# A dense layer whose first three token tiles share one pass over the weights, with float64 weights decoded in that pass

## The chip, the core and the metric

The kernel runs on one core of one Trainium2 chip. A core has five engines that each work through their own queue in order: TensorE (PE, whose weight loads are shown apart as PEld), VectorE (DVE), ScalarE (ACT), GpSimd (POOL) and SyncE (SP), which here only issues DMAs. They wait for each other by semaphores. The metric is the device time of one execution in microseconds (us).

## The reference, cut to what matters

```python
attn_out = _attn_ref(q, k, v)                    # 4 x 8 heads x 576 x 64, two sparse masks
x = attn_out.transpose(0, 2, 1, 3).reshape(2304, 512)
# experts: each token with x @ w_skip > 0 goes to the one expert with the largest logit
for e in range(8):                               # w1: 8 x 512 x 1024, w2: 8 x 1024 x 512, float32
    h = np.maximum(xc[mask] @ w1[e], 0.0)
    y[mask] = gate_w[mask, None] * (h @ w2[e])
out[do_compute] = xc + y
# dense layer, all 2304 tokens; w_in 512 x 2048 and w_out 2048 x 512 are float64
h = x @ w_in
g = np.maximum(0.01 * h, h)
return (g @ w_out).astype(np.float32)
```

## The kernel before, in words

The program has three stages: attention with the router, the experts, and the dense layer.

**Products.** Every float32 operand of a product is split into a high part (type fp32r) and a low part (the rest), and three products are added: high by high, high by low, low by high. One step of an expert or of the dense layer takes 128 hidden columns (a chunk f) and 256 tokens. `mm1` makes the hidden values `ph` in PSUM from 12 products of 256 columns, and `mm2` adds 6 products of 512 columns into the outputs `po` (experts) or `pf` (dense layer). PE's order is written by hand: `mm1` of step j, then `mm2` of step j - 2 (LAG = 2). `ph` has two buffers, so `mm1` of step j + 2 can't begin before the readers of `ph` of step j are done.

**Experts.** An expert has 8 chunks, so there are 64 steps. For each step SP loads a piece of w1 and of w2 (256 KB each). ACT makes the high parts (L495, L504), DVE the low part of w1 (`l1`, L498) and POOL the low part of w2 (`l2`, L507). Of `ph`, ACT makes `gh` (L596) and DVE makes `gl` (L597, which reads `ph` in PSUM and `gh` in SBUF). `split_rows` turns the 256 token rows of the next expert once per expert. `expert_out` adds the result to the rows (L602) and POOL scatters them to memory (L604); POOL also gathers the rows (L541). `last_out` passes the last expert's part straight into the dense layer's first rows.

**Decoding.** The dense weights are float64 and are turned into float32 parts on the chip. There are 64 jobs, four for each of the 16 chunks of the dense layer (two of w_in, two of w_out), in the chunks' order. A job has four steps: SP loads 256 KB (`raw`, three buffers); ACT takes the absolute of the high words into `w` (L128, two buffers); DVE does four operations on `w` (L133 to L136); ACT copies the high part (L141) and POOL subtracts it for the low part (`lo`, L142). Each call of `decode_tick` moves every job under way by one step and lets a new one enter. Six jobs enter during attention. The other 58 enter beside the experts, one in each step from the third on (`DEC_MOE`), and `decode_ready(15)` finishes them all ahead of the dense layer.

**Dense layer.** Nine tiles of 256 tokens are done one after the other, 16 steps each, so the weights are gone through nine times. In a step, ACT makes `t = 0.01 ph` (L737), DVE `g = max(t, ph)` (L739), ACT `gh` (L742) and DVE `gl = g - gh` (L743, where `g` and `gh` both lie in SBUF). The rows of the next tile are loaded in its fifth step and split in its tenth.

The order on the engines other than PE is set by the scheduler of the language, with the first operation of each decode step put behind the PE instruction that stands there in the program.

## Time and profile before

| what | us |
|---|---|
| median of 3 runs (lowest to highest) | 868.01 (867.65 to 873.32) |
| span of the profiled execution, first to last instruction | 859.5 |
| median of the runs less that span | 8.5 |
| attention and router | 192.3 |
| experts, to the dense layer's first product | 253.1 |
| dense layer and last outputs | 414.1 |

The profile is of one execution. Its page gives busy time by engine over the whole span, and the views named below give it by stage, by line and in order of time. Busy time alone doesn't say what a stage waits for: an engine that is busy can be held by another in the middle of an instruction, and then the duration of that instruction is long. So the durations of one kind of instruction are given both as a mean and as lowest, median and highest.

### The profile page before, as it was taken

The numbers are of one execution on the slowest core, as the hardware profiler recorded it, in microseconds if no ns is written. First come the engines' busy times: TensorE is split into PE (matmuls) and PEld (weight loads), VectorE is DVE, ScalarE is ACT, GpSimd is POOL, SyncE is SP. The second block draws the span as 40 slices with busy tenths as digits, with TensorE's granted clock in tenths as the row PEclk, the third lists the DMA queues.
The fourth block names the chain that finished last, engine by engine and source line by source line (L and its number), as shares of the span: only waits on it lengthen the run. The fifth ranks groups of instructions, "written<-read, shape, count | busy, mean of one in ns | idle before, by whom it ended". The sixth has DMA issues, their size and how long they took to land.

```text
span 859.5 us, 14337 instructions
## 1 busy us (share of the span) xinstructions
PE 768.2 (89%) x5090; PEld 681.4 (79%) x5090; DVE 473.3 (55%) x1247; ACT 359.3 (42%) x940; POOL 184.8 (21%) x203
## 2 busy tenths in 40 slices
PE   7885699859888788788889999999999999999998
PEld 6874599838766666676669899999999999999897
DVE  3552187758999999999973323232323232323222
ACT  5453165636465465565543333333333333333322
POOL 0010001125676676676640000000000000000000
PEclk9897688979999999999999999999999999999999
DMA  8994389768766676676521000000000000000000
GB/s 203 229 224 131 117 213 236 205 171 262 219 215 206 208 225 209 201 226 209 179 78 49 24 25 26 26 25 26 25 26 25 25 1 25 1 25 2 24 2 25
DMA packets 83108, 98.28 MB, mean 114 GB/s; under 512 B 8124, under 2 KB 55790, under 8 KB 83029
## 3 DMA queue, kind: packets, MB, share of 16 engines
q1 hardware_dynamic: 80468, 93.12, 37.4%
q0 software_dynamic: 2560, 4.18, 1.6%
q8 instruction: 41, 0.67, 0.3%
q14 instruction: 39, 0.31, 0.1%
HBM read 85.41 MB, written 16.09 MB: 118 GB/s over the span
## 4 chain that ended last, share of the span: by engine, by line
PE 58%; DVE 19%; DMA 14%; issue 5%; ACT 2%; POOL 1%; SPq 1%; DVEq 0%; ACTq 0%; POOLq 0%
PE ph L583 25%; PE pf L591 23%; DVE l L498 4%; DMA tt<-in_tl 4%; DMA xs_d<-xo 4%; DVE w L135 3%; PE sc L284 3%; DVE w L133 3%; DVE w L134 2%; DVE w L136 2%; DVE gl L597 2%; PE o L318 2%; DMA kb<-x_d,idx 2%; PE po L591 1%; DMA qb<-in_qs 1%
## 5 line engine op out<-in xcount | busy, mean ns | idle before, releaser
L739 DVE TENSOR_TENSOR g<-t,ph 128x256 f32<-128x256 f32 x144 | 60.6, 421 | 200.1 <-ACT t L737 200.0
L583 PE MATMUL ph<-th,winh 128*128 128x256 f32 x576 | 161.8, 281 | 0.2 <-ACT th L574 0.2
L583 PE MATMUL ph<-tl,winh 128*128 128x256 f32 x576 | 161.0, 280 | 0.3 <-DVE tl L575 0.3
L583 PE MATMUL ph<-th,winl 128*128 128x256 f32 x576 | 160.4, 278 | 0.0
L737 ACT ACTIVATE t<-ph 128x256 f32<-128x256 f32 x144 | 55.3, 384 | 205.4 <-PE ph L583 205.3
L591 PE MATMUL pf<-woutl,gh 128*128 128x512 f32 x288 | 114.1, 396 | 0.0
L591 PE MATMUL pf<-wouth,gl 128*128 128x512 f32 x288 | 114.1, 396 | 0.0
L591 PE MATMUL pf<-wouth,gh 128*128 128x512 f32 x288 | 113.7, 395 | 0.0
L583 PEld LDWEIGHTS ph<-tl,winh 128*128 128x128 f32 x576 | 108.1, 188 | 6.7 <-DVE tl L575 0.5
L583 PEld LDWEIGHTS ph<-th,winh 128*128 128x128 f32 x576 | 108.4, 188 | 6.3 <-ACT th L574 0.4
L583 PE MATMUL ph<-th,h 128*128 128x256 f32 x256 | 77.5, 303 | 37.9 <-DVE gl L597 37.3
L583 PEld LDWEIGHTS ph<-th,winl 128*128 128x128 f32 x576 | 108.3, 188 | 0.0
L743 DVE TENSOR_TENSOR gl<-g,gh 128x256 fp32r<-128x256 f32 x144 | 61.2, 425 | 70.0 <-PE pf L591 54.3
L583 PEld LDWEIGHTS ph<-th,h 128*128 128x128 f32 x256 | 49.3, 193 | 55.4 <-DVE gl L597 54.0
L507 POOL TENSOR_TENSOR l<-r,h 128x512 fp32r<-128x512 f32 x64 | 88.3, 1380 | 18.2 <-ACT h L504 5.0
L742 ACT CAST gh<-g 128x256 fp32r<-128x256 f32 x144 | 58.5, 407 | 66.2 <-DVE g L739 66.2
L583 PE MATMUL ph<-tl,h 128*128 128x256 f32 x256 | 73.2, 286 | 0.3 <-DVE tl L521 0.3
L583 PE MATMUL ph<-th,l 128*128 128x256 f32 x256 | 73.0, 285 | 0.0
L498 DVE TENSOR_TENSOR l<-r,h 128x512 fp32r<-128x512 f32 x64 | 60.6, 947 | 10.9 <-ACT h L495 6.1
L284 PE MATMUL sc<-kb,qb 128*96 128x128 f32 (+2 forms) x344 | 56.4, 316 | 9.4 <-DMA qb<-in_ql 3.5
L591 PEld LDWEIGHTS pf<-wouth,gl 128*128 128x128 f32 x288 | 54.1, 188 | 13.0
L290 ACT ACTIVATE p_t<-sc,mx 96x128 f32<-96x128 f32 (+2 forms) x172 | 48.6, 365 | 25.7 <-DVE mx L287 25.2
(116 smaller groups left out, 1422.8 us busy)
## 6 DMA issues: line engine op xcount, KB each, us to landing
r<-in_w SPq DMA_DIRECT2D x128, 256.0 KB
raw<-in_win SPq DMA_DIRECT2D x32, 256.0 KB
raw<-in_wout SPq DMA_DIRECT2D x32, 256.0 KB
kb<-x_d SPq DMA_DIRECT2D x18, 256.0 KB
out<-y SPq DMA_DIRECT2D x18, 256.0 KB
x_d<-xt SPq DMA_DIRECT2D x11, 384.8 KB
vt<-in_vl SPq DMA_DIRECT2D x12, 296.0 KB
kb<-in_kl SPq DMA_DIRECT2D x12, 256.0 KB
```

Of the source, the lines that this page charges most:

```text
L133: behind_pe(nc.vector.tensor_scalar(wf, wf, F32_MAX_HI, F32_MIN_HI, ALU.min, ALU.max))
L135: nc.vector.scalar_tensor_tensor(w, raw[:, :, 1], 0xC0000000, w, ALU.bitwise_and, ALU.bitwise_or)
L284: nc.tensor.matmul(sc[:, h, :], z["q"][:, h, :nq], z["k"][:, h, :], start=True, stop=True)
L290: nc.scalar.activation(p_t[:nq, h, :nk], sc[:, h, :], AF.Exp, bias=mx[:, h:h + 1], scale=scale)
L498: nc.vector.tensor_tensor(l1, r1, h1.bitcast(F32), ALU.subtract)
L507: nc.gpsimd.tensor_tensor(l2, r2, h2.bitcast(F32), ALU.subtract)
L583: nc.tensor.matmul(ph, a[:, c, :], x[:, c, :], start=(i == 0), stop=(i == n - 1))
L591: nc.tensor.matmul(po[t], a[:, s], x, start=(first and i == 0), stop=(last and i == 2))
L737: nc.scalar.mul(t1, ph, 0.01)
L739: nc.vector.tensor_tensor(g, t1, ph, ALU.max)
L742: nc.scalar.copy(gh, g)
L743: nc.vector.tensor_tensor(gl, g, gh.bitcast(F32), ALU.subtract)
```

## The change

The dense weights are held in one tile per chunk instead of one tile for all. The tiles of the first 8 chunks stand from the beginning; those of the last 8 are laid into the memory that the experts' tiles leave free. Only 16 of the 58 jobs enter beside the experts, one in every fourth step; the other 42 enter in the dense layer. There the first three token tiles go together: four steps of tile 0 come first (LEAD), and then each round has one step of tile 0, one of tile 1 and one of tile 2, the latter two four chunks behind. In the 48 steps of these tiles `decode_tick` is called once, once and twice in turn, so four jobs enter in a round of three steps, as many as one chunk needs. Tile 2 adds its outputs in the PSUM buffers that otherwise serve the row splits; the rows of tiles 1 and 2 are loaded at the beginning of the dense layer and split after its fourth step, one behind the other, and those of tile 3 are split in the buffers of `ph`. Tiles 3 to 8 run one after the other as before.

```diff
-DEC_MOE = set(range(2, 64))
-DEC_F = 15
+DEC_MOE = set(range(2, 64, 4))
+DEC_DENSE = (1, 1, 2)
+TRIO = 3
+EC = 8
+LEAD = 4
...
+    def weight_tiles(pool, lo, hi):
+        for n, nm in enumerate(("winh", "winl", "wouth", "woutl")):
+            for f in range(lo, hi):
+                dense_w[n, f] = pool.tile([P, KC, P] if n < 2 else [P, DM], F32R, tag=f"{nm}{f}", name=nm)
+
+    weight_tiles(big, 0, EC)
...
-    def split_rows(rows):
-        th = mp.tile([P, KC, NTT], F32R, tag="th", name="th")
-        tl = mp.tile([P, KC, NTT], F32R, tag="tl", name="tl")
+    def split_rows(rows, pool=ps_c, tag="c"):
+        th = tp.tile([P, KC, NTT], F32R, tag="th", name="th")
+        tl = tp.tile([P, KC, NTT], F32R, tag="tl", name="tl")
...
-    decode_ready(DEC_F)
...
+    ectx.close()
+    late = ctx.enter_context(tc.tile_pool(name="late", bufs=1, reuse_waits=RW))
+    weight_tiles(late, EC, FC2)
...
-    fseq = [(i, f) for i in range(NI) for f in range(FC2)]
+    fseq = [(0, f) for f in range(LEAD)]
+    for r in range(LEAD, FC2 + LEAD):
+        fseq += [(i, r if i == 0 else r - LEAD) for i in range(TRIO) if i or r < FC2]
+    n_trio = len(fseq)
+    fseq += [(i, f) for i in range(TRIO, NI) for f in range(FC2)]
+    rows = {i: load_rows(i) for i in range(1, TRIO)}
...
-                pos[i] = [ps_a.tile([P, DM], F32, tag="a", name=f"pf{t}") for t in range(2)]
-            if i == 0:
-                decode_ready(min(f + DEC_F, FC2 - 1))
+                pool, tag = (ps_c, "c") if i == TRIO - 1 else (ps_a, "a")
+                pos[i] = [pool.tile([P, DM], F32, tag=tag, name=f"pf{t}") for t in range(2)]
+            decode_ready(f)
...
+            if j == LEAD - 1:
+                for n in range(1, TRIO):
+                    xt_of[n] = split_rows(rows.pop(n))
...
+            if j < n_trio:
+                for _ in range(DEC_DENSE[j % len(DEC_DENSE)]):
+                    decode_tick()
```

On DVE, in the middle of the experts before (`l` the low part of w1, `gl` that of the hidden values, `w` the four operations of a decode job), two steps read:

```order
L498 TENSOR_TENSOR l_3708<-r_3613,h_3707 128x512
L597 SCALAR_TENSOR_TENSOR gl<-ph,gh 128x256
L133 TENSOR_SCALAR w<-w 128x256
L134 TENSOR_SCALAR w<-w 128x256
L135 SCALAR_TENSOR_TENSOR w<-raw,w 128x256
L136 SCALAR_TENSOR_TENSOR w<-raw,w 128x256
L498 TENSOR_TENSOR l_3753<-r_3658,h_3752 128x512
L597 SCALAR_TENSOR_TENSOR gl<-ph,gh 128x256
```

The same engine and stage of the change, over three steps:

```order
L141 TENSOR_SCALAR w<-w 128x256
L509 TENSOR_TENSOR l_4001<-r_3916,h_4000 128x512
L142 TENSOR_SCALAR w<-w 128x256
L608 SCALAR_TENSOR_TENSOR gl<-ph,gh 128x256
L143 SCALAR_TENSOR_TENSOR w<-raw,w 128x256
L144 SCALAR_TENSOR_TENSOR w<-raw,w 128x256
L509 TENSOR_TENSOR l_4036<-r_3961,h_4035 128x512
L608 SCALAR_TENSOR_TENSOR gl<-ph,gh 128x256
L509 TENSOR_TENSOR l_4087<-r_3996,h_4086 128x512
L608 SCALAR_TENSOR_TENSOR gl<-ph,gh 128x256
```

A job stood in nearly every step; now one stands in every fourth.

On DVE in the dense layer before, two steps (`g` the hidden values, `gl` their low part) read:

```order
L739 TENSOR_TENSOR g<-t_6277,ph 128x256
L743 TENSOR_TENSOR gl_6282<-g,gh_6281 128x256
L739 TENSOR_TENSOR g<-t_6298,ph 128x256
L743 TENSOR_TENSOR gl_6303<-g,gh_6302 128x256
```

The same engine in the shared pass of the change, about two steps:

```order
L758 TENSOR_TENSOR g<-t_6462,ph 128x256
L142 TENSOR_SCALAR w<-w 128x256
L143 SCALAR_TENSOR_TENSOR w<-raw,w 128x256
L762 TENSOR_TENSOR gl_6467<-g,gh_6466 128x256
L144 SCALAR_TENSOR_TENSOR w<-raw,w 128x256
L141 TENSOR_SCALAR w<-w 128x256
L142 TENSOR_SCALAR w<-w 128x256
L143 SCALAR_TENSOR_TENSOR w<-raw,w 128x256
L758 TENSOR_TENSOR g<-t_6499,ph 128x256
L144 SCALAR_TENSOR_TENSOR w<-raw,w 128x256
L141 TENSOR_SCALAR w<-w 128x256
L762 TENSOR_TENSOR gl_6504<-g,gh_6503 128x256
```

Decode operations now stand between `g` and `gl` of one step and between the steps.

On SP, at the beginning of the dense layer of the change (`kb` rows of tokens out of `x_d`, `raw` float64 weights to decode):

```order
L130 DMA raw<-in_win 128x2x256
L130 DMA raw<-in_wout 128x512
L545 DMA kb_125<-x_d 128x512 x2
L545 DMA kb_126<-x_d 128x512 x2
L130 DMA raw<-in_wout 128x512
L545 DMA kb_127<-x_d 128x512
L130 DMA raw<-in_win 128x2x256
```

The four loads of the rows of tiles 1 and 2, which read what the last expert scatters, stand ahead of the next loads for decoding.

## Rows read from the trace of the kernel before

**Rows 1.** Busy time by stretch, whole stages: us, busy by engine, PEclk, DMA share, GB/s.

```profile
0.00:192.30 192.30, 147.67 (x1192) 136.17 (x1192) 101.12 (x548) 87.84 (x295) 18.11 (x52) 0.83 0.75 192
192.30:445.40 253.10, 210.14 (x1243) 174.81 (x1243) 239.48 (x396) 140.08 (x324) 165.68 (x151) 0.97 0.66 206
445.40:859.50 414.10, 410.42 (x2655) 370.39 (x2655) 132.69 (x305) 131.38 (x322) 0.97 (x1) 1.00 0.07 22
```

**Rows 2.** Waits of the experts' stage: us in total, times, longest us.

```profile
PEld ph L583 <- DVE gl L597: 54.0, 41, 3.2
```

**Rows 3.** Chain of work that ended last, dense layer: start us, us, what.

```profile
451.22 1.40 PE ph L583 x12
452.62 1.40 PE pf L591 x6
...
851.65 4.21 PE pf L591 x18
```

**Rows 4.** Groups by line, experts: busy us, mean ns, idle before with releasers.

```profile
L135 DVE SCALAR_TENSOR_TENSOR w<-raw,w 128x256 uint32<-128x256 uint32 x58 | 46.7, 805 | 1.1
...
L134 DVE TENSOR_SCALAR w<-w 128x256 uint32<-128x256 uint32 x58 | 37.6, 648 | 1.3
...
L136 DVE SCALAR_TENSOR_TENSOR w<-raw,w 128x256 uint32<-128x256 uint32 x58 | 36.2, 623 | 0.5
L133 DVE TENSOR_SCALAR w<-w 128x256 f32<-128x256 f32 x58 | 30.2, 521 | 3.8 <-ACT w L128 3.8
...
L128 ACT ACTIVATE w<-raw 128x256 f32<-128x256 f32 x58 | 25.3, 436 | 10.1 <-POOL winl L142 4.7 <-POOL woutl L142 4.2 <-DMA raw<-in_wout 0.5
...
L141 ACT CAST wouth<-w 128x256 fp32r<-128x256 f32 x30 | 12.2, 406 | 45.9 <-DVE w L136 45.9
```

**Rows 5.** Single lines, experts: ns lowest/median/highest of one, first and last start.

```profile
L133 DVE TENSOR_SCALAR w<-w x58: 275/286/2472, 202.3 to 439.1; 128x256 f32<-128x256 f32 x58
L134 DVE TENSOR_SCALAR w<-w x58: 275/296/2132, 202.6 to 439.4; 128x256 uint32<-128x256 uint32 x58
L135 DVE SCALAR_TENSOR_TENSOR w<-raw,w x58: 406/426/2467, 202.9 to 439.7; 128x256 uint32<-128x256 uint32 x58
L136 DVE SCALAR_TENSOR_TENSOR w<-raw,w x58: 407/424/2092, 203.4 to 440.7; 128x256 uint32<-128x256 uint32 x58
L498 DVE TENSOR_TENSOR l<-r,h x61: 671/684/2899, 195.2 to 426.1; 128x512 fp32r<-128x512 f32 x61
L597 DVE SCALAR_TENSOR_TENSOR gl<-ph,gh x64: 406/411/425, 195.8 to 437.7; 128x256 fp32r<-128x256 f32 x64
L507 POOL TENSOR_TENSOR l<-r,h x63: 1262/1313/1808, 198.0 to 437.6; 128x512 fp32r<-128x512 f32 x63
L142 POOL TENSOR_TENSOR woutl<-w,wouth x30: 732/748/1200, 207.0 to 441.7; 128x256 fp32r<-128x256 f32 x30
```

**Rows 6.** Timeline of DVE and POOL, in an expert: start us, us, what.

```profile
329.99 2.46 DVE L135 SCALAR_TENSOR_TENSOR w<-raw,w 128x256 uint32<-128x256 uint32 x1
...
330.19 0.75 POOL L142 TENSOR_TENSOR woutl<-w,wouth 128x256 fp32r<-128x256 f32 x1
330.88 1.27 POOL L507 TENSOR_TENSOR l<-r,h 128x512 fp32r<-128x512 f32 x1
332.37 0.41 DVE L597 SCALAR_TENSOR_TENSOR gl<-ph,gh 128x256 fp32r<-128x256 f32 x1
```

**Rows 7.** The page's costliest groups, dense layer: busy us, mean ns, idle before.

```profile
L739 DVE TENSOR_TENSOR g<-t,ph 128x256 f32<-128x256 f32 x144 | 60.6, 421 | 200.1 <-ACT t L737 200.0
...
L743 DVE TENSOR_TENSOR gl<-g,gh 128x256 fp32r<-128x256 f32 x144 | 61.2, 425 | 70.0 <-PE pf L591 54.3
```

**Rows 8.** Timeline around the dense layer's beginning, engines PE, POOL and SP.

```profile
440.21 0.61 PE L552 MATMUL pts<-zero 128*128 128x512 bf16 x2
...
446.20 0.97 POOL L604 DMA_INDIRECT x_d<-kb,idx  x1 [2.45 <-DVE tl L575]
...
448.36 2.73 SPq L534 DMA_DIRECT2D kb<-x_d  x6
```

More of the change, by code (lines that the diff above doesn't have):

```diff
@@ L98, in tile_sparse_attention_moe_ffn @@
     x2_d = dp.tile([NT, XW], F32, name="x2_d")
-    winh = big.tile([P, KC, DFF], F32R, name="winh")
-    winl = big.tile([P, KC, DFF], F32R, name="winl")
-    wouth = big.tile([P, FC2, DM], F32R, name="wouth")
-    woutl = big.tile([P, FC2, DM], F32R, name="woutl")
+    dense_w = {}
+    def weight_tiles(pool, lo, hi):
[3 more added lines that the diff above has]
+    weight_tiles(big, 0, EC)
     DN = 256
@@ L140, in decode_step @@
             wf = sh(w.bitcast(F32))
+            hi, lo = dense_w[k, f][:, cols], dense_w[k + 1, f][:, cols]
             behind_pe(nc.scalar.copy(hi, wf))
@@ L508, in split_w2 @@
         return h2, l2
-    def split_rows(rows):
-        th = mp.tile([P, KC, NTT], F32R, tag="th", name="th")
-        tl = mp.tile([P, KC, NTT], F32R, tag="tl", name="tl")
+    def split_rows(rows, pool=ps_c, tag="c"):
+        th = tp.tile([P, KC, NTT], F32R, tag="th", name="th")
+        tl = tp.tile([P, KC, NTT], F32R, tag="tl", name="tl")
         for c2 in range(KC // 2):
-            pt = ps_c.tile([P, 2, NTT], F32, tag="c", name="ptx")
+            pt = pool.tile([P, 2, NTT], F32, tag=tag, name="ptx")
             for c in range(2):
@@ L565, in last_out @@
             gys.append((yh, yl))
-        th, tl = (mp.tile([P, KC, NTT], F32R, tag=n, name=n) for n in ("th", "tl"))
+        th, tl = (tp.tile([P, KC, NTT], F32R, tag=n, name=n) for n in ("th", "tl"))
         for t in range(2):
@@ L729, in tile_sparse_attention_moe_ffn @@
             if f == 0:
-                th, tl = xt_of.pop(i)
-                pos[i] = [ps_a.tile([P, DM], F32, tag="a", name=f"pf{t}") for t in range(2)]
-            if i == 0:
-                decode_ready(min(f + DEC_F, FC2 - 1))
-            fs = slice(f * P, (f + 1) * P)
-            ph = mm1(winh[:, :, fs], winl[:, :, fs], th, tl)
-            t1 = wp.tile([P, NTT], F32, tag="h2", bufs=HB2, name="t1")
+                pool, tag = (ps_c, "c") if i == TRIO - 1 else (ps_a, "a")
+                pos[i] = [pool.tile([P, DM], F32, tag=tag, name=f"pf{t}") for t in range(2)]
+            decode_ready(f)
+            ph = mm1(dense_w[0, f], dense_w[1, f], *xt_of[i])
+            if f == FC2 - 1:
+                xt_of.pop(i)
+            t1 = wp.tile([P, NTT], F32, tag="t1", bufs=HB2, name="t1")
             nc.scalar.mul(t1, ph, 0.01)
-            g = wp.tile([P, NTT], F32, tag="l2", bufs=HB2, name="g")
+            g = wp.tile([P, NTT], F32, tag="g", bufs=HB2, name="g")
             nc.vector.tensor_tensor(g, t1, ph, ALU.max)
-            gh = mp.tile([P, NTT], F32R, tag="gh", bufs=3, name="gh2")
-            gl = mp.tile([P, NTT], F32R, tag="gl", bufs=3, name="gl2")
+            gh = wp.tile([P, NTT], F32R, tag="gh", bufs=3, name="gh2")
+            gl = wp.tile([P, NTT], F32R, tag="gl", bufs=3, name="gl2")
             nc.scalar.copy(gh, g)
@@ L744, in tile_sparse_attention_moe_ffn @@
             gs[j] = gh, gl
-            if i + 1 < NI and f == 4:
-                rows[i + 1] = load_rows(i + 1)
         if j >= LAG:
@@ L757, in tile_sparse_attention_moe_ffn @@
                         for b in (1, 0):
-                            mm2(po, *gs[j - LAG - b], wouth[:, f - b, :], woutl[:, f - b, :], False, b == 0, (t,))
-                    y = wp.tile([P, DM], F32, tag=("h1", "l1")[t], bufs=HB, name="y")
+                            mm2(po, *gs[j - LAG - b], dense_w[2, f - b], dense_w[3, f - b], False, b == 0, (t,))
+                    y = wp.tile([P, DM], F32, tag=f"y{t}", bufs=2, name="y")
                     nc.scalar.copy(y, po[t])
@@ L763, in tile_sparse_attention_moe_ffn @@
             i, f = fseq[j]
-            if i + 1 < NI and f == 9:
-                xt_of[i + 1] = split_rows(rows.pop(i + 1))
+            if j == LEAD - 1:
+                for n in range(1, TRIO):
+                    xt_of[n] = split_rows(rows.pop(n))
+            if i >= TRIO - 1 and i + 1 < NI and f == 4:
+                rows[i + 1] = load_rows(i + 1)
+            if i >= TRIO - 1 and i + 1 < NI and f == 9:
+                xt_of[i + 1] = split_rows(rows.pop(i + 1), *((ps_b, "b") if i < TRIO else (ps_c, "c")))
+            if j < n_trio:
+                for _ in range(DEC_DENSE[j % len(DEC_DENSE)]):
+                    decode_tick()
 def _layout(inputs):
```

18 lines of the change are left out of this document (10 added, 8 removed).

## Prediction

> **What bounds the kernel now.** I read the busy time by stretch first, cut at the experts' first product and at the dense layer's [rows 1]. The dense layer is PE's: 410.4 of 414.1 us busy at the full clock. The experts are not: PE is busy for 210 of 253 us, and DVE for 239.5. The list of waits says the same: the weight load of `mm1` waits 54.0 us for `gl` [rows 2], an operation of DVE that frees the buffer of `ph`.
>
> Next, what PE needs where nothing holds it. In the dense layer a step takes 1.40 + 1.40 = 2.80 us [rows 3]. From the first product at 445.4 to 855.9 are 410.5 us, which is 144 steps (403.2 us) and 8 row splits, so a split costs 0.9 us. A step in an expert has the same 12 and 6 products, yet it takes 253.1/64 = 3.95 us.
>
> Then, why DVE is so busy. The groups by line give the four operations of a decode job as 521 + 648 + 805 + 623 ns = 2.60 us [rows 4], the single lines as 286 + 296 + 426 + 424 = 1.43 us by the median, with single ones up to 2.47 us [rows 5]. The timeline shows what happens in the long ones: L135 begins at 329.99 and ends at 332.45, and while it runs POOL does a `lo` and an `l2`, to 332.15; it ends 0.30 us after them [rows 6]. So DVE is held while POOL works, not slow. This befalls operations that take all operands from SBUF (L133 to L136, and `l1`, 0.68 us, up to 2.90) and not `gl`, which reads PSUM: 64 of them lie between 406 and 425 ns [rows 5].
>
> If those operations of DVE and POOL's subtractions can never run together, the experts need 64 x (0.684 + 1.313) + 58 x (1.432 + 0.748) = 127.8 + 126.4 = 254 us. The stage takes 253. I read this as its bound: not DVE alone, but DVE and POOL taking turns.
>
> **The change part by part.**
>
> *Experts.* Of 58 jobs about 15 stay. The turns come to 127.8 + 15 x 2.18 = 160.5 us, and PE's own work is longer: 64 x 2.80 = 179.2, 7 splits 6.3, and `last_out` from 440.2 to 445.4 [rows 8], 5.2: together 190.7 us. What remains of the wait for `gl` isn't shown anywhere: nothing at best; if it goes by the number of jobs, 54.0 x 15/58 = 14 us. DVE's order has three steps without a job behind one with a job, in which it can catch up, so I take the middle, 7. The stage is then 197.7 us, or **-55.4** (bounds -62.4 and -48.4).
>
> The loads don't take over: the stage moves 206 GB/s x 253.1 us = 52.1 MB now [rows 1], 43 jobs of 0.262 MB go away, and 40.8 MB in 197.7 us are 206 GB/s again, at which the DMA engines are busy for 0.66.
>
> *The shared pass.* A round of three steps needs 8.40 us of PE. DVE has three `g` and `gl` (421 and 425 ns, [rows 7]) and four jobs. Its price has two ends. Were DVE never held, it would be 3 x 0.846 + 4 x 1.43 = 8.26 us, hidden below PE's 8.40. Held as often as in the experts, it would be 2.54 + 4 x 2.60 = 12.9 us. Between them lies the turn-taking: four jobs with their `lo`, 4 x 2.18 = 8.72, and three `gl`. In the dense layer `gl` has both operands in SBUF, as `l1` has, so I count it as held too: + 1.28 = 10.0 us. `g` reads PSUM and goes beside POOL. I take 10.0, since this count gave the experts' 253 us. In the experts POOL's subtractions come to 2.06 us a step, the most of it in pieces of 1.31; here they are one of 0.75 us per job, so the price is nearer to the taking of turns than to 12.9.
>
> The Trainium skill ("SBUF — State Buffer", section "Who interferes with whom") says that a DVE instruction with two SBUF inputs waits for the whole of a GpSimd instruction that reads SBUF, and one with a single SBUF input doesn't. The rows of `l1` and of the experts' `gl` agree (2899 against 425 ns at most, [rows 5]); no run here shows the dense `gl` beside POOL. With the rule a round is 10.0 us, without it for `gl` 8.72, which over the pass would be 12 us less.
>
> 39 of the 44 jobs that DVE still has at the beginning fall into such rounds, 9.75 rounds. PE can't run ahead of DVE, because `mm1` waits for `g` two steps back. So the cost is 9.75 x (10.0 - 8.4) = **+15.6** (bounds 0 and 9.75 x 4.5 = +43.9). Behind the last job the steps go at 2.80 again.
>
> ACT is no bound: three `t` and `gh` and four times 0.436 + 0.406 [rows 4] are under 6 us a round. The weights are in time by the order of jobs: at the step that first needs chunk f, the jobs that have entered are seven past that chunk's last.
>
> *The beginning of the dense layer.* SP's loads of the rows of tiles 1 and 2 stand behind the last scatter, which POOL issues at 446.2; SP issues them at 448.4, 3.0 us after the first dense product [rows 8]. The rows are split after four steps of tile 0, some 8 us in, so they arrive in time, if barely. Behind them on SP stand loads for decoding, and on ACT `t` of the fourth step stands behind what such a load feeds. Two splits follow one another and need the same two PSUM buffers, and the rows of tile 3 are split in `ph`'s, which holds the next `mm1`. None of this can be read off a row; between 1 us and 9 (three times a wait of a step), I take **+5**.
>
> Tiles 3 to 8, attention and the number of products are the same: nothing.
>
> *Sum*, against the profiled execution: 859.5 - 55.4 + 15.6 + 5 = 824.7 us. The median of the runs lies 8.5 us above that span, so **833 us**.
>
> **The rivals.**
>
> *A. DVE isn't held in the shared pass.* POOL's `lo` comes when DVE is at `g`. Then the round is PE's 8.4 us and the time 833 - 15.6 = 818. For it: POOL has only 3.0 us of work in a round. Against it: DVE has something to do all the time, and most of it is of the kind that is held.
>
> *B. DVE is held in the pass as often as in the experts.* Round 12.9 us, + 28 us on the forecast: 861, too near to 868 to be told from it with much confidence. For it: the mean of 58 jobs. Against it: POOL's operations are fewer and shorter there.
>
> *C. The experts find another bound below 3.95 us a step.* POOL has gathers and scatters in its one queue, which wait for each other's landing, and `l2` stands behind them. At 3.2 us a step instead of 2.9 (its 165.7 us less 43 x 0.75 are still 133 us), the stage keeps 19 us: 852. For it: POOL's queue is in order. Against it: two thirds of the stage's new length is a load that leaves room.
>
> *D. It gets slower: the jobs in the shared pass go one at a time.* `w` has two buffers, and ACT's next Abs waits for `lo`, then stands in front of `t`. If this chain doesn't overlap, a job costs 0.436 + 1.43 + 0.406 + 0.748 = 3.02 us and a quarter of DVE's 2.54 us for the products, 3.66; a round 14.6 us; and the pass loses 9.75 x 6.2 = 61 us, more than the experts gain: 859.5 - 55.4 + 61 + 5 + 8.5 = 878. It decides from a round of 8.4 + 50.4/9.75 = 13.6 us on. Against it: with two buffers the DVE part of one job can lie beside the copy and `lo` of the one before.
>
> **How the numbers follow.** The forecast has 0.54, A 0.14, B 0.12, C 0.14, D 0.06. The range from 817 to 856 holds the forecast with most of its bounds, A and C; B and D, 0.18, are left out. A measurement of this kernel tells about 1% from no change, so faster is below 859: the forecast, A and C, 0.82. B is within 1%, D is slower, with a little of B: 0.11 and 0.07.
>
> **What would show it.** In the changed profile: the experts' stage at some 198 us with the wait of `mm1` for `gl` down from 54 us to under 15, and steps near 2.9 us; the shared pass (48 steps) at some 158 us instead of 137, with `mm1` waiting for `g` and PE busy for about five sixths; L141 to L144 with medians as now and means between 1.4 and 2.2 us a job in the pass; tiles 3 to 8 at 2.80 us a step. The prediction is wrong if the experts stay above 3.2 us a step, or if a round takes under 8.8 or above 12 us.

## The result and the profile after

The changed kernel takes 840.9 us in the median of its first four runs and before 870.2 on the same chip: 0.964 of before, 95% interval 0.957 to 0.971. The slowest of the four, 846.5 us, of which the first profile is, ran slow at a lower granted clock (0.925, the others 0.936 to 0.943), and it counts in that median but neither in the ratio nor in the ranges below. Two further sets of runs gave 0.962 [0.957, 0.966] and 0.963 [0.959, 0.967]. It is faster by 3.6 to 3.8%; forecast were 833 us, 0.960 of the 868.0 shown.

The first profile of it spent 202.4 us ahead of the experts. A second one, of the same kernel, is read here; its stages are cut as in [rows 1] (at the first product of the experts, and 0.7 us behind the first of the dense layer).

Busy time by stretch, kernel after, second profile (us, busy time by engine, granted clock, DMA share, GB/s):

```profile
0.00:198.94 198.94, 163.01 (x1193) 152.94 (x1193) 101.44 (x548) 88.04 (x294) 18.82 (x52) 0.74 0.73 185
198.94:404.44 205.50, 195.70 (x1244) 174.44 (x1243) 142.40 (x220) 114.44 (x237) 127.85 (x105) 0.99 0.66 201
404.44:830.20 425.76, 415.87 (x2655) 375.04 (x2655) 200.56 (x481) 162.66 (x410) 37.31 (x46) 1.00 0.14 47
```

The experts' stretch is 47.6 us shorter than in [rows 1]; PE is now busy in 95% of it, and DVE in 69% (95% before). The dense layer is 11.7 us longer, with PE busy in 98% of it (99% before).

Waits of PE's products in the experts' stretch (us in total, times, longest), kernel before:

```profile
PE ph L583 <- DVE gl L597: 37.3, 34, 2.8
PE po L591 <- POOL l L507: 4.1, 7, 1.2
```

and after, second profile:

```profile
PE po L602 <- POOL l L518: 5.7, 4, 2.4
PE ph L594 <- DVE gl L608: 3.4, 5, 0.9
```

The 54.0 us of [rows 2] are those of the weight loads (PEld), which wait for the same `gl`; they are 5.4 us now, and the products' wait fell from 37.3 to 3.4. The wait that is now the largest, for `l2` (POOL's subtraction), isn't new: it was 4.1 us before, in seven short pieces, and is 5.7 now, with single ones up to 2.4.

Waits of the same kernel, from 404.4 to 530 us, the beginning of the dense layer with the shared pass:

```profile
PE ptx L529 <- DVE tl L532: 1.9, 1, 1.9
PE ptx L529 <- DVE g L758: 1.8, 2, 1.6
PE ph L594 <- DVE tl L532: 1.3, 1, 1.3
PE ph L594 <- DVE g L758: 1.1, 5, 0.4
```

Five of these 6.1 us belong to the splits of tiles 2 and 3 (1.9 + 1.8 + 1.3), and only 1.1 to the products that wait for DVE.

The stages of all kernels, from their profiles, with the run's median (or single time) beside; the kernel before that ran beside each stands in the last column:

| kernel | experts | dense | time | before |
|---|---|---|---|---|
| before [rows 1] | 253.1 | 414.1 | 868.0 | |
| after, first profile | 214.1 | 428.2 | 840.9 | 870.2 |
| after, second (`after_again`) | 205.5 | 425.8 | 832.7 | 865.0 |
| after, third (`changed_beside`) | 212.1 | 427.2 | 836.8 | 869.7 |
| `lo_on_dve` | 243.3 | 414.1 | 856.4 | 865.0 |
| `decode_moved_alone` | 208.9 | 472.1 | 876.2 | 865.0 |
| `l2_on_dve` | 199.9 | 428.8 | 828.6 | 865.0 |
| `none_beside_experts` | 200.8 | 450.8 | 854.1 | 869.1 |
| `low_parts_zeroed` | 210.7 | 422.1 | 833.0 | 869.1 |
| `splits_apart` | 208.5 | 420.7 | 831.5 | 869.1 |
| `pad_32_bytes` | 210.1 | 429.3 | 840.2 | 869.1 |
| `tokens_elsewhere` | 253.3 | 414.1 | 871.0 | 869.7 |
| `weights_cut` | 253.1 | 414.0 | 867.4 | 871.7 |
| `both_mended` | 200.8 | 421.3 | 822.8 | 869.7 |

The experts of one and the same code (the second and third profile of the changed kernel, and `low_parts_zeroed`, `splits_apart`, `pad_32_bytes`, which leave them alone) differ by 6.6 us, from 205.5 to 212.1; the dense layer of one code by 3.5 (425.8 to 429.3). Effects below that are taken from waits and durations, not from stage times.

### The profile page after: what moved, and what is told of

Read it like the earlier page. It is cut to its first block, busy times and chain, and to the rows that moved or that the text cites. A ratio compares the mean times of both kernels' runs of the same rounds, so it can differ in the third digit from the quotient of the medians.

```text
span 844.7 us, 14324 instructions
## 1 busy us (share of the span) xinstructions
PE 783.0 (93%) x5090; PEld 709.4 (84%) x5090; DVE 443.9 (53%) x1247; ACT 366.0 (43%) x940; POOL 184.1 (22%) x203
## 4 chain that ended last, share of the span: by engine, by line
PE 56%; DVE 13%; issue 3%; DMA 2%; POOL 2%; ACT 1%; SPq 0%; DVEq 0%; POOLq 0%; ACTq 0%
PE ph L594 28%; PE pf L602 19%; PE po L602 8%; DVE w L143 3%; DVE w L142 3%; DVE w L144 2%; PE ptx L529 1%; DMA r<-in_w 1%; DVE w L141 1%; DVE l L509 1%; POOL l L518 1%; DVE gl L762 1%; DVE g L758 1%; DMA raw<-in_wout 1%; DVE kb L613 0%
## 5 line engine op out<-in xcount | busy, mean ns | idle before, releaser
L594 PE MATMUL ph<-th,winh 128*128 128x256 f32 x576 | 164.2, 285 | 2.3 <-DVE tl L532 1.3
L594 PE MATMUL ph<-tl,winh 128*128 128x256 f32 x576 | 163.6, 284 | 0.3 <-DVE tl L586 0.3
L594 PE MATMUL ph<-th,winl 128*128 128x256 f32 x576 | 163.5, 284 | 0.0
L594 PEld LDWEIGHTS ph<-tl,winh 128*128 128x128 f32 x576 | 110.6, 192 | 5.6 <-DVE tl L586 0.5
L509 DVE TENSOR_TENSOR l<-r,h 128x512 fp32r<-128x512 f32 x64 | 64.1, 1001 | 67.3 <-ACT h L506 67.3
L518 POOL TENSOR_TENSOR l<-r,h 128x512 fp32r<-128x512 f32 x64 | 84.6, 1328 | 52.2 <-ACT h L515 37.3
L594 PE MATMUL ph<-th,h 128*128 128x256 f32 x256 | 74.0, 289 | 6.1 <-DVE gl L608 6.1
L293 PE MATMUL sc<-kb,qb 128*96 128x128 f32 (+2 forms) x344 | 64.3, 347 | 13.5 <-DMA qb<-in_ql 5.2
L293 PEld LDWEIGHTS sc<-kb,qb 128*96 128x96 f32 (+2 forms) x344 | 55.6, 230 | 15.3 <-issue 10.5
L602 PEld LDWEIGHTS pf<-wouth,gh 128*128 128x128 f32 x288 | 54.9, 191 | 7.0
```

The costliest lines, as they stand in the source:

```text
L293: nc.tensor.matmul(sc[:, h, :], z["q"][:, h, :nq], z["k"][:, h, :], start=True, stop=True)
L509: nc.vector.tensor_tensor(l1, r1, h1.bitcast(F32), ALU.subtract)
L518: nc.gpsimd.tensor_tensor(l2, r2, h2.bitcast(F32), ALU.subtract)
L594: nc.tensor.matmul(ph, a[:, c, :], x[:, c, :], start=(i == 0), stop=(i == n - 1))
L602: nc.tensor.matmul(po[t], a[:, s], x, start=(first and i == 0), stop=(last and i == 2))
```

## The experiments

**The changed kernel again.** No edit.

> The changed kernel, unchanged, profiled again. In the profiled execution of it that was read first, the attention stage (its code is that of before) took about 10 us more than in before, at a lower granted clock: 202.4 us to the first product of the experts where before had 192.3. Theory: this is the execution, not the change; here the stage lies within 4 us of 192.3 (but for some 3 us that the later start of the experts' first weight loads costs), and the experts take 210 to 214 us, the dense layer 425 to 428 us, as in the first reading. Rival: the change itself slows the attention stage (its tiles lie elsewhere in memory); then it is again above 199 us. The step of the experts and of the dense layer: 2.82 us was read, 2.80 before. If that belongs to the execution, it is 2.80 here; if it belongs to where the operands now lie, it is 2.82 again.

The stage ahead of the experts took 198.9 us, between the two expectations. Kernels with the code of before there took 196.1 (`decode_moved_alone`), 198.0 (`lo_on_dve`), 198.5 (`weights_cut`) and 201.8 us (`tokens_elsewhere`), so 192.3 is the lowest of the five profiles of that code and not the rule; the third profile of the changed kernel has 195.3. A slower stage by the change is not shown: the two groups overlap, though eight profiles of kernels built on the changed one (without its first) lie some 2 us higher in the mean, 199.5 against 197.3. The step of the dense layer is 2.82 us again: that does belong to the changed kernel.

**Do DVE and POOL work in turns?** In the kernel before:

```diff
-            nc.gpsimd.tensor_tensor(lo, wf, hi.bitcast(F32), ALU.subtract)
+            nc.vector.tensor_tensor(lo, wf, hi.bitcast(F32), ALU.subtract)
```

> The kernel before, with one change: the low part of a decoded weight (L142, 748 ns on POOL) is subtracted on DVE. DVE gets 58 operations more beside the experts (some 0.42 us each, as L136, +24 us), POOL 58 fewer (-43 us). Theory of the prediction (DVE and POOL work in turns, each of their operations on SBUF waits for the other's): the experts' time follows the sum of the two engines, 64 x (0.684 + 1.313) + 58 x (1.43 + 0.42) = 235 us where it was 253, so the kernel takes about 850 us, 2% faster, although DVE, the engine that the products wait for, has more to do. Rival (DVE's own throughput is the bound, with its stretched times as they are): 24 us more, about 892 us. Second rival (the bound is a latency in a job's chain of engines): within 5 us of 868.

0.986 of before [0.980, 0.991], the experts 243.3 us instead of 253.1. DVE has 58 operations more and the stage is shorter: DVE's own work can't have been the bound. The latency of a job's chain, the second rival, should have left the time within 5 us; it fell by 8.6 (865.0 to 856.4). The size is 10 us where 18 were expected. The low part of w1 in the kernel before, experts' stretch:

```profile
L498 DVE TENSOR_TENSOR l<-r,h 128x512 fp32r<-128x512 f32 x62 | 59.2, 955 | 5.8 <-ACT h L495 5.8
```

Groups of DVE by line in this kernel, between 215 and 430 us, to be held against that line and the means of [rows 4]:

```profile
L498 DVE TENSOR_TENSOR l<-r,h 128x512 fp32r<-128x512 f32 x55 | 38.5, 701 | 0.0
L133 DVE TENSOR_SCALAR w<-w 128x256 f32<-128x256 f32 x55 | 31.7, 576 | 0.0
L135 DVE SCALAR_TENSOR_TENSOR w<-raw,w 128x256 uint32<-128x256 uint32 x54 | 27.0, 500 | 0.7
L142 DVE TENSOR_TENSOR winl<-w,winh 128x256 fp32r<-128x256 f32 x27 | 20.1, 744 | 0.0
```

With POOL's `lo` gone, L135 fell from 805 to 500 ns and L498 from 955 to 701; L133 rose from 521 to 576. The moved operation takes 744 ns (`winl`) and not some 420, because POOL's `l2` still meets it: by the timelines of both engines, the 18 of the 54 in this window (`winl` and `woutl`) that begin while POOL subtracts take 1.15 us in the mean, the other 36 take 0.51. So DVE is held by POOL, as the theory says, but the sum of turns is not exact: it gave 254 us for 253 and 235 for 243.

**The decoding moved, nothing shared.** In the kernel before:

```diff
-DEC_MOE = set(range(2, 64))
-DEC_F = 15
+DEC_MOE = set(range(2, 64, 4))
+DEC_F = 1
```

> The kernel before with one part of the change alone: only 16 of the jobs are decoded beside the experts, and the other 42 or so just ahead of the chunk that needs them in the dense layer, whose first tile alone runs over the weights then (no sharing). Theory (a job costs DVE about 2 us in the pass, wherever the pass is): the experts shorten by the same 39 us as in the changed kernel, and the first tile's pass, 16 steps with 2.6 jobs each, is bound by DVE: 42 x 2.0 + 16 x 0.85 = 98 us where it was 45; so 868 - 39 + 53 = about 882 us, slower than before by 1 to 2%. Rival (jobs without the experts' splits beside them are short, 1.43 us of DVE): 42 x 1.43 + 14 = 74 us, so 858, faster than before without any sharing.

876.2 us, 1.010 of before [1.004, 1.016]: slower by 1%, within 6 us of what was expected. Busy time by stretch, experts, 100 us of the dense layer's beginning, the rest:

```profile
196.12:405.00 208.88, 196.59 (x1244) 173.98 (x1243) 142.14 (x220) 113.99 (x236) 129.23 (x106) 0.98 0.65 195
405.00:505.00 100.00, 75.24 (x283) 57.34 (x284) 90.36 (x212) 48.70 (x122) 34.41 (x45) 0.70 0.41 132
505.00:877.10 372.10, 368.44 (x2373) 332.17 (x2372) 117.34 (x271) 117.67 (x288) 0.73 (x1) 1.00 0.06 19
```

The experts get as much shorter as in the changed kernel. In the first tile's pass DVE is busy for 90 of 100 us, PE waits for weights (22.6 us in 14 waits for ACT's `winh`), and the clock granted to it falls to 0.70. The dense layer is 58 us longer, with sharing 12 to 15: three tiles over one pass give PE the work that covers the decoding. That is where the change's gain is made.

**What is left in the experts: POOL's queue.** A timeline of POOL, then of PE, kernel after (second profile):

```profile
254.37 1.57 POOL L615 DMA_INDIRECT x_d<-kb,idx  x1 [0.62 <-DVE kb L613]
255.97 0.91 POOL L151 TENSOR_TENSOR woutl<-w,wouth 128x256 fp32r<-128x256 f32 x1
256.85 1.28 POOL L518 TENSOR_TENSOR l<-r,h 128x512 fp32r<-128x512 f32 x1
261.55 1.01 POOL L615 DMA_INDIRECT x_d<-kb,idx  x1 [3.41 <-DMA x_d<-kb,idx]
262.59 2.51 POOL L518 TENSOR_TENSOR l<-r,h 128x512 fp32r<-128x512 f32 x2
```

PE in the same stretch:

```profile
263.91 0.50 PE L602 MATMUL po<-l,gh 128*128 128x512 f32 x1 [2.42 <-POOL l L518]
```

The second scatter of this expert waits 3.41 us for the first to land; the `l2` behind it in POOL's queue starts at 262.59, and PE waits for it until 263.91. PE alone in the 8 us around the wait (us, busy time, granted clock, DMA share, GB/s):

```profile
260.00:268.00 8.00, 5.58 (x28) 0.79 0.50 147
```

From 240 to 260 us and from 268 to 275 the clock is 1.0: behind the wait the products run at the lower of the two levels (1.2 of 2.4 GHz) for a while, so the 2.42 us cost some 1.7 us more (0.21 x 8). Not every wait does that: behind one of 1.74 us for `l2`, at 365.4 us, the clock stays at 1.0. The edit, in the changed kernel:

```diff
-            spl2[j - 1] = split_w2(raw2.pop(j - 1), j - 1 <= GS)
+            spl2[j - 1] = split_w2(raw2.pop(j - 1), j - 1 <= GS,
+                                   nc.vector if j > FC1 and (j - 1) % FC1 in (1, 2) else None)
```

(`split_w2` takes the engine that subtracts as a third argument, POOL if none is given.)

> The changed kernel, but the low part of w2 (L518) of two chunks of each expert, those whose subtraction stands behind the two scatters in POOL's queue, is made on DVE: 14 of 64. In the changed kernel the second scatter waited up to 4.7 us in POOL's queue, and the products waited 7.5 us in all for l2 behind it; the granted clock fell after the two longest of these waits. Theory (the queue's position is the cause): these waits go, and with them the low clock behind, 7 to 11 us: the experts take 203 to 207 us instead of 214. Rival (what is left of the experts' loss is the decoding on DVE): DVE gets 14 x 0.7 = 10 us more work, the wait for gl grows from 4.5 us, and the experts take 214 us or more.

The experts' stretch of this kernel by busy time:

```profile
198.44:398.30 199.86, 194.48 (x1244) 172.90 (x1243) 143.59 (x234) 114.40 (x237) 105.72 (x91) 1.00 0.68 208
```

and its waits:

```profile
PE po L602 <- POOL l L518: 2.1, 4, 0.7
PE ph L594 <- DVE gl L608: 1.6, 4, 0.5
PE po L602 <- DVE l L518: 0.8, 3, 0.4
```

The experts take 199.9 us (200.8 in `both_mended`, with the same edit), 5.6 to 12.2 less than in the profiles with the changed kernel's experts, and the waits are half: `l2` 2.9 us on both engines together, `gl` 1.6. DVE had 14 operations more and the wait for it shrank, so the decoding on DVE, the rival, is not what was left. POOL also had 14 subtractions fewer, which this run doesn't separate from their place in the queue; in the next run POOL has 12 operations fewer while every `l2` keeps its place, and 4.8 us of waits for it stay. That makes the queue's position the likelier cause. The whole time is 0.958 [0.953, 0.963] against 0.962 in the same set, too close to tell by itself.

**No job beside the experts.** In the changed kernel:

```diff
-DEC_MOE = set(range(2, 64, 4))
-DEC_DENSE = (1, 1, 2)
+DEC_MOE = set()
+DEC_DENSE = (1, 2, 1)
```

> The changed kernel with no job beside the experts (16 before) and one or two more per round in the shared pass, 58 jobs there. Theory (of the experts' 14 us above the prediction, the waits for POOL's l2 behind the scatters come from the queue alone and stay, 5 to 7 us; the waits for gl, 3.4 us, come from the jobs): the experts take 199 to 203 us with l2 waits of 5 us or more left and gl waits under 1 us. In the dense layer the first four steps wait for 10 jobs more than they do now, of some 2 us each less what the products cover, 10 to 14 us, and the pass, four jobs for three steps as before, runs at 8.7 to 9.3 us: the dense layer takes 438 to 445 us, so the kernel is 5 to 12 us slower. Rival (the jobs also cause the waits for l2, by holding POOL): the experts take 196 to 198 us and no wait for l2 is left.

Busy time by stretch, experts and beginning of the dense layer:

```profile
200.60:401.40 200.80, 193.67 (x1244) 173.26 (x1243) 106.88 (x165) 105.69 (x208) 116.44 (x93) 1.00 0.66 190
401.40:450.00 48.60, 32.70 (x154) 26.77 (x155) 36.81 (x91) 21.99 (x55) 13.67 (x18) 0.75 0.46 145
```

The largest wait of each of the two, of the second one up to 545 us:

```profile
PE po L602 <- POOL l L518: 4.8, 7, 1.2
...
PE ph L594 <- ACT winh L150: 14.8, 4, 6.5
```

Without a single job the experts keep 4.8 us of waits for `l2`, seven of them, none above 1.2 us: the queue makes them without the jobs. With 16 jobs the longest is 2.4 us; but the kernel before, with a job in nearly every step and longer steps, has none above 1.2 either, so that the jobs lengthen them is not shown. The kernel takes 0.983 of before's median where the changed one takes 0.962 to 0.964, a loss of some 17 us where 5 to 12 were expected: the waits ahead of the first steps are about those expected, 14.8 us for 10 to 14, but the clock of 0.75 through 48.6 us was not counted. PE was busy for 17.0 us of the two pieces at half clock (409.28 to 426.35 and 433.17 to 440.00 us), so it cost some 8.5. The rounds of the pass took 9.16 us, within the 8.7 to 9.3 expected. The sixteen jobs cost 5 to 11 us beside the experts (205.5 to 212.1 against 200.8) and 21 to 25 in the dense layer (450.8 against 425.8 to 429.3): beside the experts they are well placed.

**Is DVE held in the shared pass?** In the changed kernel, for the jobs of the dense layer:

```diff
-            nc.gpsimd.tensor_tensor(lo, wf, hi.bitcast(F32), ALU.subtract)
+            nc.gpsimd.memset(lo.bitcast(F32), 0.0)
```

> The changed kernel, but in the dense layer's shared pass POOL does not subtract the low part of a decoded weight (L151, which reads two tiles of SBUF and met L143 of the next job each time); it writes zeros there instead, so the low parts of the weights decoded in the dense layer are left out. In the changed kernel L143 took 873 ns in the pass where 426 is its time alone, and three steps took 8.72 us on average (8.46 where no engine was waited for). Theory (L143 is held by L151 for some 0.45 us a job, and this is all that the holding costs in the pass): L143 falls to 0.42 us, DVE's busy time in 428 to 503 us from 72.8 to about 58 us, and the pass gains at most the 0.26 us by which three steps exceed 8.46, some 3 us in all. Rival (the prediction's 0.75 us of holding per job, of which the records hide a part): L143 falls by 0.45 us all the same, but other operations on DVE shorten too (gl below 0.42, L144 below 0.41). Third possibility: L143 stays at 0.87 us; then it isn't L151 that it waits for.

Groups of DVE by line in the pass, 75 us of it, the changed kernel:

```profile
L143 DVE SCALAR_TENSOR_TENSOR w<-raw,w 128x256 uint32<-128x256 uint32 x34 | 29.7, 873 | 1.2
L762 DVE TENSOR_TENSOR gl<-g,gh 128x256 fp32r<-128x256 f32 x25 | 10.5, 421 | 0.0
```

and this one:

```profile
L143 DVE SCALAR_TENSOR_TENSOR w<-raw,w 128x256 uint32<-128x256 uint32 x35 | 14.8, 422 | 0.7
```

The same stretches by busy time, the changed kernel:

```profile
428.00:503.00 75.00, 74.15 (x468) 65.78 (x467) 72.75 (x185) 44.36 (x118) 26.56 (x33) 1.00 0.37 119
```

and this one:

```profile
433.00:508.00 75.00, 75.00 (x479) 68.02 (x478) 63.37 (x194) 44.93 (x124) 0.00 (x0) 1.00 0.40 119
```

POOL writes all its zeros between 408 and 419 us, so in this stretch it does nothing (x0). L143 falls by 0.45 us, nothing else on DVE shortens, DVE goes from 97 to 84% of the pass (63.4 us, not the 58 expected; more operations fit in, 194 for 185) and PE from 74.15 us to all of it. The products that begin a round in the changed kernel, by its timeline:

```profile
478.01 0.39 PE L594 MATMUL ph<-th,winh 128*128 128x256 f32 x1 [0.18 <-DVE g L758]
486.91 0.39 PE L594 MATMUL ph<-th,winh 128*128 128x256 f32 x1 [0.17 <-DVE g L758]
```

Five of its rounds take 8.90 us like this one (486.91 - 478.01), each with a short wait for `g`, those ahead of them 8.46; in the kernel with the zeros every round takes 8.46 but the one with tile 3's split. The holding is real, 0.45 us a job, and the rounds paid some 2 us for it (5 x 0.44). The round with tile 3's split is shorter too, 10.57 us for 13.18 by the same starts; together that is 4.8 us, of which 3.7 are left over the 48 steps of the three tiles (141.2 us against 144.9), since the beginning took longer here. The dense layer, 422.1 us, is 3.7 to 7.2 below that of the changed kernel, where some 3 at most were expected.

**The splits of tiles 2 and 3.** Timeline of PE, kernel after, at tile 3's split:

```profile
504.71 0.66 PE L529 MATMUL ptx<-ident,kb 128*128 128x128 f32 x4 [0.18 <-DVE g L758]
507.01 0.66 PE L529 MATMUL ptx<-ident,kb 128*128 128x128 f32 x4 [1.64 <-DVE g L758]
508.99 0.39 PE L594 MATMUL ph<-th,winh 128*128 128x256 f32 x1 [1.32 <-DVE tl L532]
```

It takes turns with `ph` for the same two buffers: its halves wait for `g`, which reads a `ph` there (0.18 and 1.64 us), and the next `ph` waits for `tl`, which reads the half before it (1.32). The edit:

```diff
-            if j == LEAD - 1:
-                for n in range(1, TRIO):
-                    xt_of[n] = split_rows(rows.pop(n))
+            if LEAD - 1 <= j < LEAD + TRIO - 2:
+                xt_of[j - LEAD + 2] = split_rows(rows.pop(j - LEAD + 2))
...
-            if i >= TRIO - 1 and i + 1 < NI and f == 9:
-                xt_of[i + 1] = split_rows(rows.pop(i + 1), *((ps_b, "b") if i < TRIO else (ps_c, "c")))
+            if i >= TRIO - 1 and i + 1 < NI and f == (13 if i < TRIO else 9):
+                xt_of[i + 1] = split_rows(rows.pop(i + 1), *((ps_a, "a") if i < TRIO else (ps_c, "c")))
```

> The changed kernel; the tokens of tile 3 are split at the chunk 13 of tile 2 through the accumulators that tile 0 has left, instead of at chunk 9 through the two buffers in which the products ph of the pass take turns, and tile 2 is split one step after tile 1 instead of right behind it. Theory (these two places cost what the products wait there, 1.89 us for tile 2's split and 0.18 + 1.64 + 1.32 us for tile 3's): 4 to 5 us of waiting go, and the dense layer takes 421 to 423 us instead of 426.5. Rival (DVE is full in the pass, so the splits only push the waits to the next g): the waits return at other places, and the dense layer takes 425 us or more.

The dense layer takes 420.7 us, 5.1 to 8.6 less than in the kernels with that code, and the waits named are gone. They were worth 5 us, as the waits say; 2 of these go in `low_parts_zeroed` too, where one wait of 1.0 us is left at tile 3's split, so the two gains don't add up.

**The step of 2.82 us.** Three edits, each with one difference between the two kernels. In the changed one, 32 bytes ahead of the large tiles:

```diff
+    pad = const.tile([P, 8], F32, name="pad")
+    nc.vector.memset(pad, 0.0)
     zero = const.tile([P, P], BF16, name="zero")
```

> The changed kernel with a pad of 32 bytes a partition ahead of the large tiles, so that the weights and the tokens' tiles th and tl, which lay 32 bytes past a multiple of 64, lie on multiples of 64. In before, th and tl lay on a multiple of 64 and the weights 32 bytes past one; its products L583 of a step took 1.40 us. In the changed kernel th and tl lie 32 bytes past one as well, and the products L594 take 1.43 to 1.44 us. Theory (where the operand that streams through lies costs 2%): L594 takes 1.40 us again, a step 2.80 instead of 2.82 to 2.83, and over 208 steps the kernel is 4 to 6 us faster, about 827 us. Rival (the difference has another cause, such as the cut of the weights into tiles of one chunk): 1.43 us again, no change.

In the kernel before, the line that opens the pool `mp` (of `th`, `tl`, `gh` and `gl`) ahead of that of `rw`:

> The kernel before, with the pool of the tokens' tiles (th, tl, gh, gl) opened ahead of the two pools of the experts' weights: th and tl lie 35 KB lower in each partition, at 171 instead of 206 KB, still on multiples of 64 bytes, and nothing else is changed. In the changed kernel they lie at 105 KB, and the products of a step take 1.43 us where before had 1.40; the pad showed that the offset of 32 bytes isn't the cause. Theory (the place of th and tl in the partition is the cause): L583 takes more than 1.41 us in the dense layer. Rival (the cause is another): 1.40 us, as in before. In any case the sum changes by at most 6 us.

In the kernel before, `winh`, `winl`, `wouth` and `woutl` as lists of one tile per chunk:

```diff
-    winh = big.tile([P, KC, DFF], F32R, name="winh")
+    winh, winl, wouth, woutl = ([big.tile([P, KC, P] if n < 2 else [P, DM], F32R, tag=f"{nm}{f}", name=nm)
+                                 for f in range(FC2)] for n, nm in enumerate(("winh", "winl", "wouth", "woutl")))
```

> The kernel before with one more part of the change alone: the dense layer's weights lie in one tile per chunk (as in the changed kernel) instead of one tile per matrix, so that the four blocks of a chunk that a step loads lie 512 bytes apart in a partition and not 8 KB. In every kernel with this cut so far the products of a step in the dense layer (mm1, then mm2) took 1.43 + 1.39 us, in every one without it 1.40 + 1.40; neither the 32 bytes of offset nor the place of th and tl made the difference. Theory (the cut does it): 1.43 us for L581 in the dense layer after its first tile, the dense layer 3 to 4 us longer than the 414.8 us of before. Rival (another cause, such as the tiles th and tl in four buffers): 1.40 us, the dense layer 414 to 415 us. The experts are as in before, 252 us.

Weight loads of `mm1` in the dense layer behind the pass (mean ns, the last number ahead of the second bar): kernel after, then `pad_32_bytes`, `tokens_elsewhere` and `weights_cut`:

```profile
L594 PEld LDWEIGHTS ph<-th,winh 128*128 128x128 f32 x376 | 71.8, 191 | 3.9
```

```profile
L596 PEld LDWEIGHTS ph<-th,winl 128*128 128x128 f32 x378 | 72.2, 191 | 0.0
```

```profile
L583 PEld LDWEIGHTS ph<-th,winh 128*128 128x128 f32 x352 | 66.2, 188 | 3.7
```

```profile
L581 PEld LDWEIGHTS ph<-th,winl 128*128 128x128 f32 x352 | 66.2, 188 | 0.0
```

191 ns stays 191 and 188 stays 188; a step is 1.43 + 1.39 us in every kernel built on the changed one and 1.40 + 1.40 in every one built on before. All three theories fell, each alone. One more row narrows it: in the experts, whose code for the weights is the same, a step that waits for nothing takes 2.81 us in the changed kernel and 2.80 in `decode_moved_alone`, so neither the cut nor the order of the jobs is needed for it. That `th` and `tl` now have four buffers was not tried. What makes the 0.02 us, some 3 us over the dense layer's 144 steps, stays open.

**Both mendings together**, `l2_on_dve` and `splits_apart`, beside the changed kernel on one chip:

> The changed kernel with the two mendings that were looked at apart: the l2 of the 14 chunks behind a scatter on DVE, and the splits of tiles 2 and 3 at other places (the pad is left out). Theory (the two are independent: one lies in the experts, the other in the dense layer): the experts take 199 to 201 us and the dense layer 421 to 422 us; from the 830.2 us of the changed kernel's second profile, 4 to 6 us less in the experts and 5 less in the dense layer, so about 820 us, 1.0 to 1.3% below the changed kernel that runs beside it. Rival (the waits that go in one place come back in another): within 4 us of the changed kernel.

> The changed kernel, unchanged, on the same chip as the mended one, so that the two can be compared. Expected: 830 to 842 us, as in its runs so far, and 0.960 to 0.968 of before.

Experts, then dense layer; first the mended kernel, then the changed one:

```profile
202.53:403.30 200.77, 194.34 (x1243) 172.85 (x1243) 143.87 (x234) 114.36 (x237) 106.38 (x91) 1.00 0.69 206
403.30:824.60 421.30, 415.69 (x2655) 374.83 (x2655) 199.62 (x481) 162.65 (x410) 36.94 (x46) 1.00 0.15 48
```

```profile
195.31:407.40 212.09, 198.70 (x1243) 176.78 (x1243) 144.26 (x220) 114.31 (x237) 126.93 (x106) 0.98 0.66 198
407.40:834.60 427.20, 417.35 (x2655) 376.29 (x2655) 200.78 (x481) 162.72 (x410) 37.06 (x46) 1.00 0.15 47
```

822.8 us against 836.8, 0.947 of before [0.942, 0.952] against 0.963 [0.959, 0.967]: 1.7% below the changed kernel, the intervals apart. In the two profiles the experts are 11.3 us shorter, where 4 to 6 were foreseen (this changed kernel stands at the upper end of its own 205.5 to 212.1), and the dense layer 5.9, where 5 were; the stage ahead of the experts, left alone, was 7.2 us longer. It beats both kernels.

## Why the prediction was right, and where its steps were not

The time fell where it was forecast, in the likeliest case and on the side named, but the sum is right because two terms were wrong in opposite directions: that part is luck. All differences here are against [rows 1].

- *What bounds the experts: right in kind.* DVE is held by POOL (`lo_on_dve`: more work for DVE, 10 us less time; `low_parts_zeroed`: L143 873 ns with POOL's `lo`, 422 without), and with 42 jobs gone PE is the bound: busy for 195.7 of 205.5 us. The wait of `mm1` for `gl` is 5.4 us in the weight loads and 3.4 in the products, where under 15 were forecast.
- *The experts' gain, -55.4 us: mis-sized.* It is -47.6 and -41.0 us in the second and third profile, outside the bounds given (-62.4 to -48.4). The term left out is rival C's: `l2` behind the scatters in POOL's queue. The prediction gave it the choice between nothing and 19 us; it was 5.7 us of waiting, and the low clock behind the longest wait on top. The kernel before had 4.1 us of waits for `l2` already, in the list that [rows 2] is from, so there was a row against nothing. Step by step from the 190.7 us of PE's own work: waits for `l2` 5.7, for `gl` 3.4 (7 had been taken), the longer step about 0.9 (64 x 0.014), the clock from 260 to 268 us 1.7; the remaining 3.1 us of the second profile are not assigned.
- *Its own signs of being wrong.* The prediction is wrong, it said, if a round takes under 8.8 us: the nine rounds that decode take 8.46 four times and 8.90 five times, 8.70 in the mean, so by this sign the pass was wrong. The other sign, experts above 3.2 us a step, depends on the count. The whole stage by 64, as in its 3.95 us, gives 3.21 to 3.31, above the mark; without the splits and `last_out` (11.5 us), as in its 2.9, it gives 3.03 to 3.13, below it. The prediction mixed the two.
- *The shared pass, +15.6 us: mis-sized by far.* Rounds of 10.0 us were forecast for 9.75 rounds; the changed kernel has 8.46 in the first ones and then five of 8.90, so the rounds pay about 2 us, and the 48 steps of the pass took 144.9 us where 158 were forecast. The durations add up to nearly the forecast: four times 0.282 + 0.287 + 0.873 + 0.415 and three `g` and `gl` of 0.409 and 0.421 come to 9.9 us. By its parts that is chance, since the jobs have 7.4 us of it instead of 8.72, and `g`, which was to go beside POOL at no cost, has 1.2. The step that failed is adding durations end to end. Timeline of DVE and POOL in the pass:

```profile
447.00 0.29 DVE L141 TENSOR_SCALAR w<-w 128x256 f32<-128x256 f32 x1
447.21 0.41 DVE L758 TENSOR_TENSOR g<-t,ph 128x256 f32<-128x256 f32 x1
447.54 0.28 DVE L142 TENSOR_SCALAR w<-w 128x256 uint32<-128x256 uint32 x1
447.86 0.85 DVE L143 SCALAR_TENSOR_TENSOR w<-raw,w 128x256 uint32<-128x256 uint32 x1
448.62 0.41 DVE L762 TENSOR_TENSOR gl<-g,gh 128x256 fp32r<-128x256 f32 x1
448.96 0.41 DVE L144 SCALAR_TENSOR_TENSOR w<-raw,w 128x256 uint32<-128x256 uint32 x1
```

```profile
447.60 0.81 POOL L151 TENSOR_TENSOR winl<-w,winh 128x256 fp32r<-128x256 f32 x1 [1.26 <-ACT winh L150]
```

L141 ends at 447.00 + 0.29 = 447.29 by its record, and `g` has begun at 447.21. In the same way `g` reaches to 447.62 (L142 begins at 447.54), L143 to 448.71 (`gl` at 448.62) and `gl` to 449.03 (L144 at 448.96): a record reaches 0.07 to 0.09 us into the one behind it, except L142's, behind which L143 is held. What an operation costs in a full queue is the distance of starts, 0.33 us for `g` and not 0.41. Over the 22 operations of the round from 478.01 us these overlaps come to 1.2 us and DVE's gaps to 0.2: that is the 1.0 us between 9.9 and 8.9. The row was there to be read: in [rows 6] `gl` begins at 332.37, and the operation ahead of it ends at 332.45.

The Trainium skill says so ("Perfetto Trace Analysis", section "Optimizing Scalar/DVE Operations"): the profiled latency of an instruction is longer than what it takes of the engine, since the acknowledgement of its write goes beside the next instruction. The trace agrees that records overlap, by 0.07 to 0.09 us here; that it is the acknowledgement, no run here shows. The prediction didn't draw on it.

- *Which operations are held: half right.* The dense `gl` was counted as held, 1.28 us a round; it takes 421 ns, as alone. One `lo` holds one operation, and in this order that is L143 (33 of the 34 from 428 to 503 us begin within a `lo`, and no other operation of DVE does), since L142 began before `lo` (447.54 against 447.60) and `gl` follows behind it. L143 begins at 447.86 within `lo`, ends 0.30 us behind it (448.71 against 448.41), and loses 0.45 us by it, not `lo`'s whole 0.75. The section of the Trainium skill that was cited ("SBUF — State Buffer", section "Who interferes with whom") also says that issue order decides who waits. That stands in the trace: L142 began first and kept its 0.28 us. Counting every operation with two such operands as held was the prediction's own step. The same section frees an instruction with one SBUF input only outside the modes that use both ports, a condition that the prediction left out; its own rows of L133 and L134, with one such input and up to 2.47 and 2.13 us [rows 5], show instructions of that kind held.
- *Rival A (rounds at PE's 8.4 us, 818 us)* was nearest for the pass, for another reason than it gave: DVE is held, and has the time for it.
- *The beginning of the dense layer, +5 us: right in size, by luck.* The waits of the splits are 1.9 + 1.8 + 1.3 = 5.0 us, and taking them away gave 5 us or more; but the 5 was a middle between 1 and 9, taken without a row.
- *Rival D (one job at a time, slower)* didn't come: DVE is 97% busy in the pass, and a round without a split takes 8.9 us at most where D had 14.6. That the decoding alone, without sharing, makes the kernel slower (876.2 us) has another reason: PE lacks work beside it.
- *"Tiles 3 to 8 the same, nothing": not quite.* 2.82 us a step instead of 2.80, about 3 us over the dense layer, cause open. With the splits (5.0) and the rounds (2.2) that makes some 10 of the 11.7 us by which the dense layer grew.
- *The sum.* For experts and dense layer together -34.8 us were forecast; the second and third profile have -35.9 and -27.9. Of the 8.5 us between the span of the profiled execution of before and the median of its runs, 1.8 lie between a run's time and its span in every run here; most of the rest lay ahead of the experts, where the other four profiles of the same code took 3.8 to 9.5 us more.

## What to carry to other kernels

Decoding that fills an engine costs least where a second engine has enough work of its own in the same stretch: the same 42 jobs made the kernel 1% slower over one tile's pass and nearly 4% faster over three. Price a full queue by the distance between the starts of its instructions, not by the durations added up. When a stage's bound goes, look next at what stands in a queue behind an instruction that waits for a transfer: such a wait is small beside the old one (4.1 us of PE's waiting against 37.3 here), and when that goes it is the largest one left, with the matrix engine's granted clock lower behind the longest piece of it.

## What the runs showed of the hardware that was not expected

- A wait of PE can cost more than itself: in the 8 us around one of 2.4 us the granted clock was 0.79, while behind one of 1.74 us it stayed at 1.0. Where several waits follow one another it is 0.70 (100 us of `decode_moved_alone`, waits up to 3.9 us) and 0.75 (48.6 us of `none_beside_experts`, up to 6.5).
- POOL's second scatter into the same tensor waited 3.41 us for the semaphore of the first one's landing, with everything behind it in POOL's queue.
- The loads of 128 x 128 weights take 191 ns in one kernel and 188 in another with the same code in that place; 32 bytes of offset, the place of the streamed operand and the cut of the weights' tile, each tried alone, make no difference.
- DVE's records overlap in a full queue, by 0.07 to 0.09 us, so that 9.9 us of records took 8.9.
